# A planned attention and two-layer-pair kernel: stores on GpSimd's queue, adding transfers, packed matmuls kept together, half-size temporaries

## The chip, the cores and the metric

One core of a Trainium2 chip runs the whole program. The metric is the time of one execution on the device in microseconds; smaller is better. Engines are named as in the profile: PE is TensorE's matmul, PEld its weight load, DVE is VectorE, ACT ScalarE, POOL GpSimd, SP SyncE, which here only issues DMAs.

## The reference

```python
scores = scale * np.matmul(x, state.transpose(0, 1, 3, 2))
a = softmax(scores)
xread = np.matmul(a, state)
scores2 = scale * np.matmul(state, x.transpose(0, 1, 3, 2))
a2 = softmax(scores2)
sread = np.matmul(a2, x)
x = concat(xread, sread), laid out as 4352 tokens of 512
h = np.maximum(x @ w1, 0.0)
x = h * h @ w2
h = x @ w3
return (h / (1 + np.exp(-h))) @ w4
```

softmax stands for the reference's lines that subtract the maximum, take exp and divide by the sum. There are 8 batches with 8 heads; x has 512 rows of 64 in each head, state has 32 (S = 512, Ns = 32). The weights are 512x2048 and 2048x512. They arrive as 64-bit floats, so each weight is read as two 32-bit words.

## The kernel before, in words

**Precision.** PE multiplies in a reduced fp32 format (fp32r). A factor is therefore split into a rounded part hi (made by ACT) and a remainder lo (made by DVE or POOL), and a product is hi·hi + hi·lo + lo·hi: three matmuls of 512 columns. Some products run in plain fp32 on a part of the array instead.

**Stage one** walks through steps (batch b, column block c). For the first three batches (NB = 3) the sixteen column blocks are done in two halves (PARTS): blocks 0 to 7 for batches 0, 1, 2, then blocks 8 to 15. Since xread is a times state, the kernel first forms G = state·w1 (`g_unit`, L579: sixteen units, each with two packs of four fp32 matmuls of 64x64 on quarters of the array), and then multiplies the softmax by G (`gemm1`, L767), applies the squared ReLU (`chain_a`), and multiplies by w2 (`gemm2`, L791). The scores of the first three batches are packs of four fp32 matmuls too (`scores`, L641, tile xTr). G for batches 0 and 1 is copied straight from SBUF to SBUF (Glo<-go); the rest of G goes to DRAM (g<-go) and is loaded later (Glo<-g). The results of stage one, combined for a Strassen-like scheme of seven products, go to DRAM as the x operands (x_d, in `evac_a`, L820: seven stores for each of nine blocks).

**Conversion of weights** (`sched_conv`, L540): 32 pairs of 512 KB loads (raw), ACT takes an absolute value (cv), DVE runs seven instructions on the bits (`c_bits`, L505), which leave two fp32 parts: c (tile cc) and a small a (tile cv). `c_sum` (L523) adds them for w1, w3 and w4. `c_split` (L533) takes c apart for w2: hi by ACT, c - hi, and then lo = that + a. The converted w1 (w1d), w3 and w4 are stored to DRAM.

**Stages two and three** (`gemm3`, L968, and `gemm4`, L1034) multiply by w3 and w4, seven products each, with the intermediate t in DRAM between them.

**The order** of all engines is written by a planner at build time (`Plan`). Every call is recorded with a cost and dependencies, and `order` (L220) simulates the engines, the free tiles and the DMA lanes, picking the next instruction by earliest start and urgency; `emit` (L371) issues in that order. So a change of costs or of a queue can move any instruction. Each engine, and SP's queue, then runs its own instructions strictly in order. Because every call passes through one recorded function, nearly all rows of the profile stand at L186, and tile names tell them apart. An operation that two engines can do (`arith` on DVE or POOL, `copy` on ACT or DVE) is recorded with `either`, and the planner chooses.

**Memory.** SBUF tiles are 50 pages of 4 KB in each partition and 10 quads of 2 KB. A page whose last reader is a store comes free when the store has landed.

Of the kernel before, what the change touches and what calls it, by code (L numbers as in the profile page):

```python
# [27 lines left out]
class Plan:  # L28
# [6 lines left out]
    LATENCY = dict(act=dict(act=153, dve=147, pool=159, pe=265, dma=0),  # L35
                   dve=dict(act=128, dve=127, pool=155, pe=256, dma=0),
                   pool=dict(act=150, dve=150, pool=150, pe=309, dma=0),
                   pe=dict(act=197, dve=196, pool=200, pe=3, dma=0),
                   dma=dict(act=0, dve=0, pool=0, pe=100, dma=0))
    LANES = 8  # L40
    WINDOW = 25
# [9 lines left out]
    def __init__(self, bufs):  # L51
        self.bufs = bufs
        self.ops = []
        self.tiles = {}
        self.seen = {}
        self.slot = 0

# [49 lines left out]
    def cost(self, eng, method, writes, reads, args):  # L107
        size = 1
        for ap in writes + reads:
            n = 1  # L110
            for d in ap.shape[1:]:
                n *= d
            size = max(size, n)
        psum = any(self.tiles.get(ap.tensor.name, (0, 0, ""))[2] == "ps" for ap in writes + reads)
        if eng == "dma":
# [26 lines left out]
    def record(self, calls):  # L142
# [45 lines left out]
        self.ops.append(dict(forms=forms, deps=deps, uses=uses, slot=self.slot, port=port))  # L188

    def urgency(self, when=None):  # L190
# [3 lines left out]
        for i, o in enumerate(ops):  # L194
            if o["forms"][0][0] == "dma":
                cost[i] += self.LEAD
        late, t = [], 0.0
        for i, o in enumerate(ops):
            if o["forms"][0][0] == "pe":
                t = when[i] + cost[i] if when else t + cost[i]  # L200
                late.append(t)
            else:
                late.append(t + (self.DSLACK if o["forms"][0][0] == "dma" else self.SLACK))
# [16 lines left out]
    def order(self, when=None):  # L220
# [26 lines left out]
        ready = {e: [] for e in now}  # L247
# [8 lines left out]
        lanes, hw, wire = [], 0.0, 0.0  # L256
        port = dict(dve=0.0, pool=0.0)
        head = 0
        busy, warm = deque(), False

# [3 lines left out]
        def earliest(i, eng):  # L264
            o = ops[i]
            e = now[eng]
# [16 lines left out]
            if eng == "dma":  # L283
                e = max(e, hw)
                if len(lanes) >= self.LANES:
                    e = max(e, lanes[-self.LANES])
# [3 lines left out]
        while done < n:  # L290
# [4 lines left out]
            for eng, cand in ready.items():  # L295
                mine = []
                low = None
                for _, i in cand[:60]:
                    if ops[i]["slot"] > limit:
                        continue  # L300
                    e = earliest(i, eng)
                    if e is None:
                        continue
                    if len(ops[i]["forms"]) > 1:
                        fin = {f[0]: (earliest(i, f[0]) + f[1] - self.FAVOR[f[0]]) for f in ops[i]["forms"]}
                        if fin[eng] > min(fin.values()):
# [3 lines left out]
                    if e <= now[eng] + self.PATIENCE[eng]:  # L310
                        break
                for e, i in mine:
                    if e <= low + self.PATIENCE[eng]:
# [16 lines left out]
            if eng == "pe":  # L330
# [4 lines left out]
                end[i] = now[eng] = e + cost * (1 if warm else 2)  # L335
                if busy and e - busy[-1][1] < 10:
                    busy[-1][1] = end[i]
                else:
                    busy.append([e, end[i]])
            elif eng == "dma":  # L340
                hw = e + 450
                now[eng] = e + 60
                wire = max(wire, e + 1100) + cost
                end[i] = wire + 1500
                lanes.append(end[i])
# [4 lines left out]
            for t in o["uses"]:  # L350
                users_left[t] -= 1
                seems = e + self.DMA_SEEMS if eng == "dma" else end[i]
# [10 lines left out]
    def best(self):  # L363
        when, found = None, None
        for _ in range(self.ROUNDS):
# [12 lines left out]
def attn_moe_moe_kernel(  # L378
# [35 lines left out]
    T, D = plan.engine("pe", nc.tensor), plan.engine("dma", nc.sync)  # L414
# [65 lines left out]
    def fire(s, phase):  # L480
        for fn, a in ev.pop((s, phase), ()):
            fn(*a)

# [39 lines left out]
    def c_sum(key, into=None):  # L523
        a, c = cv[key]
        arith(ALU.add, c, c, a)
# [4 lines left out]
    def c_store(key, dst):  # L530
        D.dma_start(dst, cv[key].rearrange("p (k n) -> p k n", k=2))

    def c_split(key, into):  # L533
        a, c = cv.pop(key)
        hi, lo = page(f"hi{key}"), page(f"lo{key}")
        split_into(hi, c, c)
        arith(ALU.add, lo, c, a)
        into[key] = (hi, lo)

    def sched_conv(key, srcs, s, into=None, dst=None, ahead=3, whole=False):  # L540
# [5 lines left out]
        else:  # L546
            at(s + 2, "vec", c_split, key, into)
# [31 lines left out]
    def g_unit(i):  # L579
# [61 lines left out]
    def scores(b, g):  # L641
# [3 lines left out]
        if b < NB:  # L645
            for l in range(2):
                for r in range(2):
                    h, ps = 2 * l + r, slice(r * 64, (r + 1) * 64)
                    T.matmul(out=t[h * NS:(h + 1) * NS], lhsT=st[ps, b // 2, 2 * g + l, b % 2],
                             rhs=x[ps, l * 512:(l + 1) * 512], start=True, stop=True, tile_position=(r * 64, h * NS))  # L650
            return
# [168 lines left out]
    def evac_a(s, j, n):  # L820
# [16 lines left out]
        for i in SEQ:  # L837
            at(s + 1, "dma", lambda i=i: D.dma_start(x_d[(i, j)].rearrange("(k p) n -> p k n", p=P), v[SRC_B[i]]))
# [195 lines left out]
    def gemm4(q):  # L1034
# [20 lines left out]

        def add(o, banks, a):
            for b in range(c):
                V.tensor_tensor(out=o[:, b], in0=banks[b], in1=a[:, b], op=ALU.add)

        def join(z, a):  # L1060
            arith(ALU.add, z, a[:, :, 0:256], a[:, :, 256:512])
# [13 lines left out]
        U = new("U4")  # L1075
        for b in range(c):
            A.copy(U[:, b], BA[b])
# [3 lines left out]
        R = new("R4")  # L1081
        for b in range(c):
            A.copy(R[:, b], BA[b])
        join(z[0][:, :, ls], R)
        prod(7, BD, True, False)
        W = new("W4")
# [5 lines left out]
        X = new("X4")  # L1092
# [143 lines left out]
    base = A_END + 2  # L1236
    for u in range(NU):
# [60 lines left out]
```

## Time and profile before

| what | value |
|---|---|
| median of 3 runs | 1383.2 us (1381.34 to 1383.8) |
| the profiled execution, its own time | 1381.88 us |
| its span, first to last instruction | 1380.1 us |
| PE busy | 1335.8 us (97%) |
| DVE, ACT, POOL busy | 1056.3, 701.0, 48.9 us |
| DMA issues from POOL | none |
| mean granted TensorE clock | 0.996 of full |

The span leaves out 1.8 us of the execution's own time around it. PE busy is the time in which some matmul is on the way; it says nothing of how much of the array it uses. In a timeline a row can stand for several instructions (x8), and the bracket holds the idle time of the engine before it and what ended it. A plain fp32 matmul shows as two records, so a pack of four shows as x8.

### The profile page before, as it was taken

What the parts mean: (1) busy time and instruction counts of PE and PEld (TensorE: products, weight loads), DVE (VectorE), ACT (ScalarE), POOL (GpSimd) and SP (SyncE); (2) the same over time, 40 slices, a digit from 0 to 9 for tenths busy, and PEclk for the clock granted to TensorE, in tenths of its full rate; (3) what the DMA queues carried; (4) which work ended last, traced back from release to release, by engine and by line L of the source; (5) the groups of instructions that cost most, each with busy time, mean ns of one, the idle gap of its engine ahead of it and who ended that gap; (6) DMA issues with size and microseconds to landing.
All of it is one profiled execution on the core that took longest, in us unless ns stands there. A gap on an engine that the chain in (4) does not pass through costs nothing. (4 is left out here: it accounts for less than half of the span.)

```text
span 1380.1 us, 19261 instructions
## 1 busy us (share of the span) xinstructions
PE 1335.8 (97%) x6892; PEld 1107.9 (80%) x6892; DVE 1056.3 (77%) x1598; ACT 701.0 (51%) x1080; POOL 48.9 (4%) x41
## 2 busy tenths in 40 slices
PE   5889999999999999999999999999998999999998
PEld 1457588888888888888988888999787888888887
DVE  6979488878898888875898866777887676665664
ACT  5755776555555646554662434244455444344442
POOL 0000001110000000000020000000111000000000
PEclk9999999999999999999999999999999999999999
DMA  8761764436264546342759956667899666665663
GB/s 302 262 244 62 223 219 131 123 120 216 80 198 127 168 144 194 112 153 107 225 177 328 363 208 233 248 233 255 280 338 362 195 215 231 220 204 187 201 205 114
DMA packets 206959, 283.08 MB, mean 205 GB/s; under 512 B 13456, under 2 KB 148112, under 8 KB 206864
## 3 DMA queue, kind: packets, MB, share of 16 engines
q1 hardware_dynamic: 206864, 281.86, 61.4%
q8 instruction: 54, 0.88, 0.3%
q14 instruction: 41, 0.34, 0.1%
HBM read 161.35 MB, written 116.26 MB: 201 GB/s over the span
## 5 line engine op out<-in xcount | busy, mean ns | idle before, releaser
L186 ACT ACTIVATE rg<-psC 128x512 f32<-128x512 f32 (+1 forms) x144 | 82.6, 574 | 199.0 <-PE psC L186 195.6
L186 PE MATMUL psC<-AThi,Ghi 128*128 128x512 f32 x256 | 101.6, 400 | 6.0 <-ACT rg L186 3.1
L186 DVE TENSOR_TENSOR gact<-rg,gact 128x512 fp32r<-128x512 f32 (+1 forms) x139 | 90.9, 656 | 19.0 <-ACT rg L186 12.8
L186 PE MATMUL psC<-ATlo,Ghi 128*128 128x512 f32 x256 | 101.1, 398 | 2.2 <-DVE ATlo L186 2.2
L186 PE MATMUL psC<-AThi,Glo 128*128 128x512 f32 x256 | 101.1, 399 | 1.7 <-DVE Glo L186 1.7
L186 ACT ACTIVATE gact<-rg 128x512 fp32r<-128x512 f32 (+1 forms) x144 | 87.7, 609 | 6.9 <-DMA g<-go 3.4
L186 DVE TENSOR_TENSOR rg<-rg 128x512 f32<-128x512 f32 (+1 forms) x66 | 43.7, 662 | 48.4 <-ACT rg L186 48.0
L186 PEld LDWEIGHTS psC<-AThi,Ghi 128*128 128x128 f32 x256 | 48.1, 188 | 21.4 <-ACT AThi L186 4.6
L186 DVE TENSOR_TENSOR W<-psD,U 128x512 f32<-128x512 f32 (+2 forms) x57 | 35.4, 631 | 35.9 <-PE psD L186 35.8
L186 PEld LDWEIGHTS psC<-AThi,Glo 128*128 128x128 f32 x256 | 48.0, 188 | 16.2 <-issue 3.3
L186 PEld LDWEIGHTS psC<-ATlo,Ghi 128*128 128x128 f32 x256 | 48.2, 189 | 14.8 <-DVE ATlo L186 2.9
L186 ACT ACTIVATE r<-r 128x1024 f32<-128x1024 f32 (+2 forms) x20 | 18.6, 932 | 73.3 <-DVE r L186 61.8
L186 DVE TENSOR_SCALAR cv<-cv 128x1024 f32<-128x1024 f32 (+1 forms) x64 | 43.4, 686 | 8.2 <-ACT cv L186 7.9
L186 ACT ACTIVATE rg<-rg 128x512 f32<-128x512 f32 (+1 forms) x78 | 46.3, 594 | 0.0
L186 DVE TENSOR_TENSOR U<-psB,U 128x512 f32<-128x512 f32 (+2 forms) x57 | 35.0, 629 | 14.1 <-PE psB L186 12.6
L186 DVE TENSOR_TENSOR W<-psC,U 128x512 f32<-128x512 f32 (+2 forms) x40 | 24.2, 609 | 27.6 <-PE psC L186 27.2
L186 ACT ACTIVATE cv<-raw 128x512 f32<-128x512 f32 x64 | 40.7, 668 | 8.9 <-DMA raw<-in_w_dram 8.9
L186 PE MATMUL psA<-cc,st 64*64 64x512 f32 x128 | 25.9, 641 | 17.7 <-DVE cc L186 17.3
L186 DVE SCALAR_TENSOR_TENSOR cc<-raw,cv 128x512 int32<-128x512 int32 x64 | 41.9, 684 | 1.4 <-DMA g<-go 1.2
L186 DVE SCALAR_TENSOR_TENSOR cv<-raw,cv 128x512 f32<-128x512 uint32 x64 | 41.5, 682 | 0.2
L186 DVE TENSOR_TENSOR Glo<-Glo,Ghi 128x1024 fp32r<-128x1024 f32 x31 | 37.7, 1216 | 1.2 <-ACT Ghi L186 1.0
L186 ACT COPY U<-psA 128x512 f32<-128x512 f32 (+2 forms) x57 | 28.9, 538 | 14.9 <-PE psA L186 14.3
(1244 smaller groups left out, 4276.2 us busy)
## 6 DMA issues: line engine op xcount, KB each, us to landing
raw<-in_w_dram SPq DMA_DIRECT2D x64, 512.0 KB, 6.4
t<-s SPq DMA_DIRECT2D x36, 512.0 KB, 5.0
Glo<-g SPq DMA_DIRECT2D x96, 128.0 KB, 4.6
t<-r SPq DMA_DIRECT2D x24, 512.0 KB, 4.6
xTr<-in_xT_dram SPq DMA_DIRECT2D x16, 512.0 KB, 8.3
g<-go SPq DMA_DIRECT2D x16, 512.0 KB, 5.7
xnr<-in_xN_dram SPq DMA_DIRECT2D x16, 512.0 KB, 5.6
x<-yt SPq DMA_DIRECT2D x32, 256.0 KB, 4.0
```

The costliest lines, as they stand in the source:

```text
L186: lambda engine=engine, method=method, a=a, k=k: getattr(engine, method)(*a, **k)))
```

## The change

- The queue: the stores of G (g_d), of converted weights (w1_d, w3_d, w4_d) and of the x operands (x_d) are issued by GpSimd (`DS`) instead of SP (`D`). Loads, the copies Glo<-go, the stores of t and of the output stay on SP. `arith` in stage one is DVE's alone; from stage two on either engine's.
- The sums: `c_sum` is a transfer from SBUF to SBUF that adds, for all pairs but w1's 3 and w2's 0. For w2, `c_sum` now runs ahead of `c_split`, which then needs one DVE instruction less.
- The packs: the four matmuls of a pack of G or scores form a group, which the planner starts when all members are ready and issues back to back; their model cost is no longer divided by the packing.
- Copies of G's units 0 to 7 out of PSUM (tile go) are ACT's alone.
- The temporaries U, R, W, X of `gemm4` are quads, one for each of the c row blocks, instead of one page; `join` is issued once for each of them.
- The planner models the second queue (1000 ns per issue).

```diff
+    DMA = ("dma", "sdma")
     LANES = 8
+    ISSUE = 1000
...
-            share = 128 * 128 // (reads[0].shape[0] * writes[0].shape[0]) if args.get("tile_position") else 1
-            return max(n / 2.4 + 13, 109) * (4 if args["rhs"].dtype == F32 else 1) / share
+            return max(n / 2.4 + 13, 109) * (4 if args["rhs"].dtype == F32 else 1)
...
-                for _, i in cand[:60]:
-                    if ops[i]["slot"] > limit:
+                for _, i in [key[m] for m in rest] if eng == "pe" and rest else cand[:60]:
+                    if ops[i]["slot"] > limit and i not in rest:
                         continue
-                    e = earliest(i, eng)
+                    g = ops[i]["group"]
+                    if g is not None and i not in rest:
+                        if any(left[m] for m in self.members[g]):
+                            continue
+                        e = max(earliest(m, eng) for m in self.members[g])
+                    else:
+                        e = earliest(i, eng)
...
-    T, D = plan.engine("pe", nc.tensor), plan.engine("dma", nc.sync)
+    T = plan.engine("pe", nc.tensor)
+
+    D, DS = plan.engine("dma", nc.sync), plan.engine("sdma", nc.gpsimd)
...
+    pool_stores = [True]
+
     def arith(op, o, a, b):
         kw = dict(out=o, in0=a, in1=b, op=op)
-        plan.either((V, "tensor_tensor", kw), (G, "tensor_tensor", kw))
+        if pool_stores[0]:
+            V.tensor_tensor(**kw)
+        else:
+            plan.either((V, "tensor_tensor", kw), (G, "tensor_tensor", kw))
...
     def c_sum(key, into=None):
         a, c = cv[key]
-        arith(ALU.add, c, c, a)
+        if key in (("w1", 3), ("w2", 0)):
+            arith(ALU.add, c, c, a)
+        else:
+            DS.dma_start(c, a, accum_op=ALU.add)
...
     def c_store(key, dst):
-        D.dma_start(dst, cv[key].rearrange("p (k n) -> p k n", k=2))
+        DS.dma_start(dst, cv[key].rearrange("p (k n) -> p k n", k=2))
 
     def c_split(key, into):
-        a, c = cv.pop(key)
+        c = cv.pop(key)
         hi, lo = page(f"hi{key}"), page(f"lo{key}")
-        split_into(hi, c, c)
-        arith(ALU.add, lo, c, a)
+        split_into(hi, lo, c)
         into[key] = (hi, lo)
...
         else:
+            at(s + 1, "vec", c_sum, key)
             at(s + 2, "vec", c_split, key, into)
...
+            plan.together = ("G", i, bp)
             for k in range(2):
                 for r in range(2):
...
+            plan.together = None
...
-                copy(o2[:, k], ts[k])
+                (A.copy if 4 * q < PARTS[0][1] else copy)(o2[:, k], ts[k])
...
-                D.dma_start(g_d[q][0][p], o2[:, 1])
+                DS.dma_start(g_d[q][0][p], o2[:, 1])
             else:
-                D.dma_start(g_d[q][1][p], o2)
+                DS.dma_start(g_d[q][1][p], o2)
 
     def w1_store(i):
-        D.dma_start(w1_d[i], w1p.pop(("w1", i)))
+        DS.dma_start(w1_d[i], w1p.pop(("w1", i)))
...
+            plan.together = ("scores", b, g)
...
-            at(s + 1, "dma", lambda i=i: D.dma_start(x_d[(i, j)].rearrange("(k p) n -> p k n", p=P), v[SRC_B[i]]))
+            at(s + 1, "dma", lambda i=i: DS.dma_start(x_d[(i, j)].rearrange("(k p) n -> p k n", p=P), v[SRC_B[i]]))
...
+        def quads_of(name):
+            return [quad(f"{name}{b}") for b in range(c)]
+
...
         def join(z, a):
-            arith(ALU.add, z, a[:, :, 0:256], a[:, :, 256:512])
+            for b in range(c):
+                arith(ALU.add, z[:, b], a[b][:, 0:256], a[b][:, 256:512])
...
-        U = new("U4")
+        U = quads_of("U4")
...
+    pool_stores[0] = False
     for u in range(NU):
```

## Rows read from the trace of the kernel before

**Rows 1.** The page: its span, and the busy time and share of each engine.

```profile
span 1380.1 us, 19261 instructions
...
PE 1335.8 (97%) x6892; PEld 1107.9 (80%) x6892; DVE 1056.3 (77%) x1598; ACT 701.0 (51%) x1080; POOL 48.9 (4%) x41
```

**Rows 2.** The table by stages: stretch, its length, then busy time by engine, clock, DMA.

```profile
0.00:35.00 35.00, 18.50 (x108) 4.88 (x108) 22.06 (x34) 19.21 (x33) 2.48 (x8) 1.00 0.82 301
...
35.00:69.00 34.00, 27.60 (x128) 15.68 (x127) 31.65 (x50) 25.32 (x45) 0.00 (x0) 1.00 0.79 262
...
69.00:138.00 69.00, 60.18 (x236) 42.75 (x235) 60.99 (x99) 36.38 (x65) 1.25 (x2) 0.95 0.41 153
...
138.00:966.00 828.00, 827.25 (x4225) 700.06 (x4225) 656.93 (x1090) 440.69 (x727) 30.71 (x23) 1.00 0.58 191
...
966.00:1104.00 138.00, 132.94 (x664) 111.06 (x662) 108.24 (x127) 69.79 (x93) 14.46 (x8) 1.00 0.86 294
...
1104.00:1380.00 276.00, 269.33 (x1541) 233.48 (x1539) 176.48 (x201) 109.58 (x123) 0.00 (x0) 0.99 0.61 197
```

**Rows 3.** PE's timeline to 140 us: start, duration, instruction, the wait before it.

```profile
14.86 1.99 PE L186 MATMUL psA<-cc,st 64*64 64x512 f32 x8 [14.86 <-DVE cc L186]
...
48.01 0.73 PE L186 MATMUL psC<-AThi,Ghi 128*128 128x512 f32 x2 [1.68 <-ACT AThi L186]
...
94.91 1.22 PE L186 MATMUL psC<-ATlo,Ghi 128*128 128x512 f32 x2 [2.21 <-DVE ATlo L186]
```

**Rows 4.** DVE's timeline to 140 us.

```profile
27.61 0.69 DVE L186 COPY go<-psB 128x512 f32<-128x512 f32 x1 [5.66 <-PE psB L186]
...
74.77 1.23 DVE L186 TENSOR_TENSOR cc<-cc,hi('w2', 2)_324 128x1024 f32<-128x1024 f32 x1 [4.20 <-ACT hi('w2', 2)_324 L186]
...
97.72 2.49 DVE L186 TENSOR_SCALAR cv<-cv 128x1024 f32<-128x1024 f32 x4
```

**Rows 5.** The waits of ACT from 45 to 100 us: total, times, longest.

```profile
ACT Ghi L186 <- DMA w1d<-cc: 2.2, 1, 2.2
...
ACT hi('w2', 2)_324 L186 <- DMA g<-go: 2.0, 1, 2.0
```

**Rows 6.** SP's timeline to 110 us: start, time for all issues of the row.

```profile
35.49 15.32 SPq L186 DMA_DIRECT2D Glo<-go  x22
...
50.85 3.94 SPq L186 DMA_DIRECT2D g<-go  x6
```

**Rows 7.** The groups of instructions on DVE, whole run, then up to 138 us: busy us, mean ns.

```profile
L186 DVE TENSOR_TENSOR cc<-cc,cv 128x1024 f32<-128x1024 f32 x24 | 29.0, 1218 | 0.1
...
L186 DVE TENSOR_TENSOR lo('w2', 1)_307<-cc,cv 128x1024 fp32r<-128x1024 f32 x1 | 1.2, 1221 | 0.0
...
L186 DVE TENSOR_TENSOR cc<-cc,cv 128x1024 f32<-128x1024 f32 x8 | 9.6, 1218 | 0.0
```

**Rows 8.** DMA issues up to 100 us: count, KB each, median us to landing.

```profile
raw<-in_w_dram SPq DMA_DIRECT2D x24, 512.0 KB, 8.1
...
Glo<-go SPq DMA_DIRECT2D x32, 64.0 KB, 2.1
```

**Rows 9.** PE's timeline again: packs of G and of scores.

```profile
25.56 1.09 PE L186 MATMUL psA<-cc,st 64*64 64x512 f32 x8
...
26.47 1.04 PE L186 MATMUL psB<-cc,st 64*64 64x512 f32 x8
...
73.14 1.04 PE L186 MATMUL psD<-xTr,st 64*32 64x512 f32 x2
...
78.33 0.50 PE L186 MATMUL psC<-AThi,Glo 128*128 128x512 f32 x1
...
79.89 1.06 PE L186 MATMUL psD<-xTr,st 64*32 64x512 f32 x8
```

**Rows 10.** The table for the second half of G alone.

```profile
139.95:158.86 18.91, 18.91 (x134) 5.90 (x133) 4.75 (x7) 14.32 (x28) 0.00 (x0) 1.00 0.65 196
```

**Rows 11.** The chain that ended last, from 940 to 1110 us.

```profile
1039.83 9.19 DMA t<-s
```

More of the change, by code (lines that the diff above doesn't have):

```diff
@@ L56, in __init__ @@
         self.slot = 0
+        self.together = None
     def tile(self, pool, shape, dt, tag, name, space="sb"):
@@ L114, in cost @@
         psum = any(self.tiles.get(ap.tensor.name, (0, 0, ""))[2] == "ps" for ap in writes + reads)
-        if eng == "dma":
+        if eng in self.DMA:
             n = 1
@@ L187, in record @@
         port = {c[0]: self.shares(c[0], writes, reads) for c in calls}
-        self.ops.append(dict(forms=forms, deps=deps, uses=uses, slot=self.slot, port=port))
+        self.ops.append(dict(forms=forms, deps=deps, uses=uses, slot=self.slot, port=port,
+                             group=self.together if eng == "pe" else None))
     def urgency(self, when=None):
@@ L194, in urgency @@
         for i, o in enumerate(ops):
-            if o["forms"][0][0] == "dma":
+            if o["forms"][0][0] in self.DMA:
                 cost[i] += self.LEAD
@@ L198, in urgency @@
         for i, o in enumerate(ops):
+            if o["group"] is not None:
+                cost[i] /= len(self.members[o["group"]])
             if o["forms"][0][0] == "pe":
@@ L202, in urgency @@
             else:
-                late.append(t + (self.DSLACK if o["forms"][0][0] == "dma" else self.SLACK))
+                late.append(t + (self.DSLACK if o["forms"][0][0] in self.DMA else self.SLACK))
         before = [list(o["deps"]) for o in ops]
@@ L246, in order @@
         now = dict(pe=600.0, act=1900.0, dve=1070.0, pool=1150.0, dma=600.0)
-        ready = {e: [] for e in now}
+        clock = dict({e: e for e in now}, sdma="pool")
+        ready = {e: [] for e in clock}
         def add(i):
@@ L259, in order @@
         busy, warm = deque(), False
+        rest, begun = [], 0.0
         def fresh(i):
@@ L265, in earliest @@
             o = ops[i]
-            e = now[eng]
+            e = begun + 7 if i in rest else now[clock[eng]]
             for d in o["deps"]:
@@ L282, in earliest @@
                 e = max(e, port["pool" if eng == "dve" else "dve"])
[L283 to L286, printed above, removed]
+            if eng in self.DMA:
+                e = max(e, hw[eng])
+                if len(lanes[eng]) >= self.LANES:
+                    e = max(e, lanes[eng][-self.LANES])
             return e
@@ L334, in order @@
                 warm = work > (1000 if warm else 2400)
-                end[i] = now[eng] = e + cost * (1 if warm else 2)
+                end[i] = e + cost * (1 if warm else 2)
+                now[eng] = max(now[eng], end[i])
+                if o["group"] is not None:
+                    rest, begun = [m for m in rest or self.members[o["group"]] if m != i], e
                 if busy and e - busy[-1][1] < 10:
-                    busy[-1][1] = end[i]
+                    busy[-1][1] = max(busy[-1][1], end[i])
                 else:
                     busy.append([e, end[i]])
[L340 to L343, printed above, removed]
+            elif eng in self.DMA:
+                issue = 450 if eng == "dma" else self.ISSUE
+                hw[eng] = e + issue
+                now[clock[eng]] = e + (60 if eng == "dma" else issue)
+                wire = max(wire, e + 650 + issue) + cost
                 end[i] = wire + 1500
-                lanes.append(end[i])
+                lanes[eng].append(end[i])
             else:
@@ L351, in order @@
                 users_left[t] -= 1
-                seems = e + self.DMA_SEEMS if eng == "dma" else end[i]
+                seems = e + self.DMA_SEEMS if eng in self.DMA else end[i]
                 last_end[t] = max(last_end[t][0], seems), max(last_end[t][1], end[i])
@@ L364, in best @@
         when, found = None, None
+        self.members = defaultdict(list)
+        for i, o in enumerate(self.ops):
+            if o["group"] is not None:
+                self.members[o["group"]].append(i)
         for _ in range(self.ROUNDS):
@@ L650, in scores @@
                              rhs=x[ps, l * 512:(l + 1) * 512], start=True, stop=True, tile_position=(r * 64, h * NS))
+            plan.together = None
             return
@@ L1080, in gemm4 @@
         prod(2, BA, False, True)
-        R = new("R4")
+        R = quads_of("R4")
         for b in range(c):
-            A.copy(R[:, b], BA[b])
+            A.copy(R[b], BA[b])
         join(z[0][:, :, ls], R)
         prod(7, BD, True, False)
-        W = new("W4")
+        W = quads_of("W4")
         add(W, BD, U)
@@ L1091, in gemm4 @@
         prod(4, BD, False, True)
-        X = new("X4")
+        X = quads_of("X4")
         add(X, BD, U)
```

21 lines of the change are left out of this document (11 added, 10 removed).

## The prediction

> **What bounds the kernel now.** I began with the page's busy shares: TensorE (PE) is busy for 1335.8 of 1380.1 us, so at most 44.3 us of idle PE time is there to win, and GpSimd (POOL) is nearly empty [rows 1]. The table by stages shows where the idle time lies. PE lacks 16.5, 6.4 and 8.8 us in the three stretches up to 138 us, 0.75 us in the 828 us behind them, 5.1 us between 966 and 1104, and 6.7 us after that, most of it the last store [rows 2]. From 138 to 966 us PE alone is the bound; there only a shorter PE stream helps. In the opening, VectorE (DVE) is the full engine: 31.65 of 34 us, then 60.99 of 69 [rows 2]. PE's own timeline names the same engine: its first matmul waits 14.86 us for the converted weights cc, and the waits at 48.01 and 94.91 end with AThi and ATlo, which stand behind DVE's work [rows 3].
>
> DVE isn't full of useful work, though. It stands still for 5.66 us before a copy of go, which the order gave to it and which waits for PE, and for 4.20 us before a subtraction that needs hi(w2,2) from ScalarE (ACT) [rows 4]. ACT was late there because a page came free only when a store of go (2.0 us), and before that a store of w1d (2.2 us), had landed [rows 5]. Those stores sat in SyncE's (SP's) queue behind 22 issues of Glo<-go that took from 35.49 to 50.85 us; the first store of go went out at 50.85 us [rows 6], long after its copy.
>
> **Part 1, the sums.** The kernel makes 24 sums cc<-cc,cv and 8 sums lo(w2)<-cc,cv on DVE, 1.22 us each [rows 7]. 30 of the 32 become adding transfers, 36.6 us of DVE time. Where PE is the bound (w3, w4 and late w2: 20 of them) this is worth nothing: PE's full rows hide it, and without that cover it would be worth the 1.22 us each. In the opening it counts: three sums of w1 and three of w2 lie ahead of the last PE wait at 94.91 us, 6 x 1.22 = 7.3 us. Four more (w1 pairs 4 to 7, the rest of the eight up to 138 us [rows 7] but pair 3) come before 138 us, 4.9 us against PE waits of about 2 us there (the rest of the 8.8 us lies ahead of 97 us): I take 2.0.
>
> What they cost has no row: no transfer here adds. From below, a 64 KB copy from SBUF to SBUF landed in 2.1 us; from above, twice the 8.1 us of a 512 KB load, since it reads both operands, 16.2 us [rows 8]. I take 8.1, the row of the same size in the same crowded stretch (DMA share 0.82 and 0.79 [rows 2]). So each sum is late by 8.1 - 1.2 = 6.9 us on two chains in turn, weights to G at the head and w2 to its products: 13.8 us if nothing covers it, 0 if DVE always has another pair's bits to work on. The next pair's steps (seven of about 0.69 us) are ready in most places, and the sums of pair 3 of w1 and pair 0 of w2 stay on DVE; I charge 4.
>
> **Part 2, stores on POOL's queue.** 119 stores (32 of go, 24 of weights, 63 of x operands) leave SP, and with the 30 sums POOL issues 149. At 1 us each (the diff's own ISSUE; SP took 15.32 us for 22, 0.7 each [rows 6]) POOL holds some 150 us of issues over 966 us, one by one: a store behind a sum that waits for DVE waits too, and so does the page that it holds. SP's queue keeps the loads and Glo<-go. The wait for pages at 74.77 us should mostly go; next late there is ACT's own queue, so I count 2.0 of the 4.20. POOL's tensor work moves to DVE: 30.71 us in 23 instructions in the stage from 138 to 966 [rows 2], under half of that on DVE, which is busy for 657 of 828 us there; hidden behind PE, cost 0. Without that cover it would be about 15 us, less than the 24 us of sums that leave the same stage.
>
> **Part 3, copies of go on ACT for the first eight units.** The stall of 5.66 us and the copy (0.69 us) leave DVE [rows 4]. ACT takes one copy more, in a stretch where it is busy for 19.21 of 35 us. Together 6.3.
>
> **Part 4, packs kept together.** A pack is four fp32 matmuls on parts of the array. Kept together, eight records of G pass in 0.91 us (25.56 to 26.47) and a pack of scores in 1.06. Where other matmuls came between, a pack of scores lasted from 73.14 to 78.33, 5.2 us: 3.4 lost, with 0.7 taken off for the other matmuls in it [rows 9]. The second half of G takes 18.91 us from 139.95, in a stretch with PE full [rows 10]; 16 whole packs at 0.91 are 14.6 and six other matmuls some 1.4, so 2.9 us are lost: I count 3.0. The pack of scores lies in the part that DVE bounds: 0 to 3.4, I take 0. A pack starts only when all four are ready, at most one copy of a bank later (0.69 us), and other products fill PE.
>
> **Part 5, half-size temporaries.** They leave six pages per round of the last product stage for two. In the chain that ended last, U waits 9.19 us for the store t<-s at 1039.83 [rows 11]; but PE lacks only 5.1 us in this whole stretch [rows 2], and loads at a DMA share of 0.86 are late next. Between 0 and 3.6, I take 1. Smaller additions cost DVE some us more after 1104, hidden behind PE (269.33 of 276 us).
>
> **The sum.** Opening: 7.3 + 6.3 + 2.0 - 4.0 = 11.6; then 2.0, 3.0 and 1.0: 17.6 us. The profiled execution took 1381.9 us and so comes to 1364.3; the median of the runs, 1383.2, is 1.3 us above it. I say 1365. PE has room for the opening's share: 31.7 - 14.9 = 16.8 us of waits behind its first matmul [rows 2, 3], the split packs, and a mean granted clock of 0.95 of its upper level, 2.4 GHz, from 69 to 138 us, where it had waited before [rows 2].
>
> **The rivals.** *Late sums* (0.22): the 13.8 us aren't covered, because DVE's order reaches a step that needs a sum and stands. Then 17.6 - 9.8 = 7.8 us remain, 1374 (1370 to 1379.5). For it: DVE has four tensor_scalar at a stretch (2.49 us [rows 4]) that POOL may have to share memory with, and the loads of the first stretch crowd the DMA engines. Against it: most of DVE's order is conversions that don't depend on each other. On this the Trainium skill (SBUF — State Buffer, "SBUF: two separate sides") says that a DMA issued from GpSimd can't have its descriptors written while such a VectorE instruction holds the shared port pair, and advises SyncE's or ScalarE's queue; no run here shows it yet. By that rule each sum would be up to 2.5 us later, and this rival gains at the forecast's cost.
>
> *Slower* (0.09): the sums take the upper bound. One mechanism: both chains late by 16.2 - 1.2 = 15 us, uncovered, 30 us against gains of 17.6 + 4 = 21.6; +8.4, 1390. It decides from a landing of 1.2 + 21.6/2 = 12 us. Only the assumption that adding doubles a transfer speaks for it.
>
> *More* (0.12): all sums covered (+4), the whole 4.20 (+2.2), the scores' pack (+3.4) and the late 2.6 more: 29.8 us, 1352 (1350 to 1358).
>
> *No effect* (0.07): the order is planned anew for the whole kernel, the freed DVE time is spent on conversions that nobody waits for, and new waits take the pack's 3 us: 1380.5 to 1386. The skill's page DMA: Bandwidth & Descriptors ("Issuing engines are not separate DMA queues") says that a second issuing engine saves only issue time. By it alone part 2 would give its 2.0 us or less; SP's 15.32 us block [rows 6] says that here the issue time is what held the stores.
>
> **How the numbers follow.** The forecast (1358 to 1370) has 0.50. The range 1353 to 1381 leaves out the slower case, most of no effect and a piece of more, together 0.2. A difference of 0.2% (2.8 us) is about what can be told from none: faster has 0.50 + 0.22 + 0.12 = 0.84, same 0.07, slower 0.09.
>
> **What would show it.** Right: PE idle up to 138 us falls from 31.7 to 25 or less though its first matmul on G comes later than 14.86 us; no copy of go on DVE before 60 us; stores of go issued before 40 us; an adding transfer landing in 5 to 10 us; scores and G in whole packs, the second half of G in some 16 us; 138 to 966 still without PE waits. Wrong: adding transfers over 12 us; PE waiting for lo(w2) or for G by several us at a time; DVE's tensor_scalar longer than 0.69 us while POOL issues; or new PE waits after 138 us.

## The result, and the profile after

| | before | changed |
|---|---|---|
| median of 4 runs, us | 1383.5 (1381.34 to 1385.19) | 1366.73 (1365.78 to 1370.45) |
| ratio | | 0.9885, 95% interval 0.9862 to 0.9908 |

By the ratio the changed kernel is faster by 15.9 us, 1.15%. It was run again as the first experiment, with a median of 1366.9, and its rows are read from that profile: the execution took 1367.0 us, at the median, while the first one profiled was the longest of its four.

First the page of the changed kernel: the span and the busy times (against [rows 1]), the queue that GpSimd's issues go to, and the adding transfers among the DMA issues (count, KB each, median us from issue to landing).

```profile
span 1365.2 us, 19493 instructions
...
PE 1323.6 (97%) x6892; PEld 1104.5 (81%) x6892; DVE 1041.7 (76%) x1637; ACT 692.8 (51%) x1067; POOL 126.7 (9%) x166
...
q0 software_dynamic: 16176, 56.50, 14.1%
...
cc<-cv POOLq DMA_DIRECT2D x30, 512.0 KB, 7.1
```

PE's idle time went from 44.3 to 1365.2 - 1323.6 = 41.6 us, 2.7 us less. The other 12.2 us of the gain in the span are PE *busy* time, although the count of matmuls is the same: the stream itself passes faster. DVE lost 36.6 us of sums and is down by only 14.6: work came back to it, 22 us in net, and what left POOL and the smaller additions are the likely part of that. POOL, busy for 48.9 us with tensors before, is now busy for 126.7 us, mostly with issues, and its queue (q0) holds the DMA engines for 14.1% of their time.

The same table by stages as [rows 2] says where:

```profile
0.00:35.00 35.00, 10.80 (x64) 2.18 (x64) 26.21 (x42) 12.06 (x19) 8.66 (x16) 1.00 0.98 344
35.00:69.00 34.00, 25.65 (x141) 12.25 (x138) 27.52 (x44) 28.23 (x53) 10.78 (x17) 0.95 1.02 344
69.00:138.00 69.00, 68.50 (x322) 51.17 (x324) 59.03 (x106) 44.87 (x78) 8.24 (x12) 1.00 0.64 177
138.00:966.00 828.00, 825.55 (x4209) 699.67 (x4199) 649.24 (x1092) 430.60 (x709) 94.33 (x118) 1.00 0.65 206
966.00:1104.00 138.00, 137.98 (x712) 117.31 (x711) 114.30 (x143) 75.37 (x95) 4.74 (x3) 1.00 0.89 297
```

Up to 138 us PE is idle for 24.2 + 8.35 + 0.5 = 33.1 us, more than the 31.7 of before. The first stretch got worse (10.80 us busy against 18.50), with DMA now full at 0.98 where it was 0.82. From 69 to 138 us PE is busy for 68.50 us and passes 322 matmuls, where it passed 236 in 60.18 [rows 2]. The mix differs (36 of the 322 are short records of G), so the counts alone mislead; with each matmul at its full-rate time (as set out below) 66.5 us of work begin in this stretch, against 51.2 before. So PE passes 0.97 us of work in a busy microsecond in place of 0.85. A pack that other matmuls split counts as busy throughout, so this gain shows in the work passed and not in the idle time; a part of it is the clock, 1.00 against 0.95 (before, PE is busy for 5.3 us at the lower of the two levels, 1.2 GHz, so some 2.7 us at most). From 966 to 1104 us the 5.1 us of idle time are gone.

PE's timeline shows the head (start, duration, tiles, and in brackets the wait before it):

```profile
11.72 3.64 PE L188 MATMUL psD<-xTr,st 64*32 64x512 f32 x16 [11.72 <-DMA xTr<-in_xT_dram]
27.49 1.93 PE L188 MATMUL psD<-xTr,st 64*32 64x512 f32 x8 [12.14 <-DMA xTr<-in_xT_dram]
29.35 1.66 PE L188 MATMUL psA<-cc,st 64*64 64x512 f32 x8
...
53.13 1.67 PE L188 MATMUL psB<-cc,st 64*64 64x512 f32 x7 [2.97 <-ACT go L188]
...
58.06 0.73 PE L188 MATMUL psC<-AThi,Ghi 128*128 128x512 f32 x2
```

G starts at 29.35 us instead of 14.86, and the first product with the softmax at 58.06 instead of 48.01 [rows 3]. The queues of SP and POOL say why:

```profile
11.60 1.74 SPq L188 DMA_DIRECT2D xTr<-in_xT_dram  x2
...
32.68 33.35 SPq L188 DMA_DIRECT2D Glo<-go  x24
```

```profile
14.36 1.06 POOL L188 DMA_DIRECT2D cc<-cv  x1 [11.26 <-DVE cv L188]
...
31.97 0.55 POOL L188 DMA_DIRECT2D g<-go  x1 [4.65 <-ACT go L188]
```

The first sum is issued at 14.36 us, into DMA engines full of loads of raw, and lands some 10 us later (the median up to 35 us is 10.1, shown with the second experiment). The new order has the scores of the next batch ahead of G on PE. Their operand xTr, issued at 11.60, lands at 27.5, and PE, which works in order, stands for 12.14 us. The first store of go, in return, leaves at 31.97 us from POOL while SP begins its Glo<-go: before, it left at 50.85 [rows 6].

**Time by equal work.** Since idle time misleads here, I compared the two traces where they have done the same work: each matmul is given the time that it needs at full rate (its columns at 2.4 GHz plus 13.5 ns, which for 512 columns is the 0.227 us at which such matmuls follow each other in the trace, and 0.11 us for a record of a fp32 pack, eight in about 0.91 us), the sums run up in the order of the matmuls' starts, and the times at which both reach the same sum are subtracted. At the sum that before had reached at 42.4 us the changed kernel is 10.7 us *behind*; at 84.2 it is 3.9 behind; at 104.3 it is 6.3 ahead and at 161.7 it is 9.1 ahead; this stays to 1014.0 (8.0 ahead); then 12.6 at 1069.1 and 15.9 at 1323.3. So the time came in two places: between 84 and 138 us, and after 1014 us.

### The profile page after: what moved, and what is told of

It reads as the page before. It is cut to its first block, busy times and chain, and to the rows that moved or that the text cites. A ratio compares the mean times of both kernels' runs of the same rounds, so it can differ in the third digit from the quotient of the medians.

```text
span 1368.7 us, 19493 instructions
## 1 busy us (share of the span) xinstructions
PE 1325.1 (97%) x6892; PEld 1104.2 (81%) x6892; DVE 1042.7 (76%) x1637; ACT 691.4 (51%) x1067; POOL 126.2 (9%) x166
## 4 chain that ended last, share of the span: by engine, by line
PE 88%; DMA 7%; ACT 1%; issue 1%; DVE 1%; SPq 1%; POOL 0%; DVEq 0%; POOLq 0%; ACTq 0%
PE psA L188 26%; PE psC L188 26%; PE psB L188 20%; PE psD L188 16%; DMA raw<-in_w_dram 3%; DMA xTr<-in_xT_dram 1%; SPq L188 1%; DMA cc<-cv 1%; DMA x44lo<-x 1%; ACT go L188 0%; DMA g<-go 0%; POOL g L188 0%; DMA w<-w4s 0%; DMA out_dram<-z 0%; DMA x47lo<-x 0%
## 5 line engine op out<-in xcount | busy, mean ns | idle before, releaser
L188 DVE TENSOR_TENSOR gact<-rg,gact 128x512 fp32r<-128x512 f32 (+1 forms) x144 | 94.3, 656 | 24.3 <-ACT rg L188 14.8
L188 DVE TENSOR_TENSOR rg<-rg 128x512 f32<-128x512 f32 (+1 forms) x73 | 49.1, 672 | 56.6 <-ACT rg L188 55.6
L188 DVE TENSOR_SCALAR cv<-cv 128x1024 f32<-128x1024 f32 (+1 forms) x64 | 44.0, 695 | 12.8 <-ACT cv L188 12.5
L188 POOL DMA_DIRECT2D cc<-cv x30 | 27.5, 919 | 259.7 <-DVE cv L188 120.9
L188 ACT ACTIVATE cv<-raw 128x512 f32<-128x512 f32 x64 | 41.1, 674 | 18.1 <-DMA raw<-in_w_dram 18.1
L188 DVE TENSOR_TENSOR U<-psB,U 128x512 f32<-128x512 f32 (+2 forms) x57 | 35.7, 629 | 14.5 <-PE psB L188 10.7
L188 ACT ACTIVATE rg<-rg 128x512 f32<-128x512 f32 (+1 forms) x71 | 41.5, 585 | 0.1
L188 ACT ACTIVATE r<-psA 128x512 f32<-128x512 f32 (+2 forms) x40 | 21.1, 535 | 31.9 <-PE psA L188 30.9
```

What stands on the lines that cost most here:

```text
L188: lambda engine=engine, method=method, a=a, k=k: getattr(engine, method)(*a, **k)))
```

## The experiments

All were timed in rounds against the kernel before. "Saved" is one minus the ratio, times the median of before in the same call. The last columns are the difference to before by equal work, in us, from the profiled executions, at the work that before had done at these times.

| run | median, us | ratio and interval | saved, us | 161.7 | 459.9 | 1069.1 | 1323.3 |
|---|---|---|---|---|---|---|---|
| e1_again | 1366.9 | 0.9887 (0.9864 to 0.991) | 15.6 | -9.1 | -8.4 | -12.6 | -15.9 |
| e2_copy_for_add | 1361.8 | 0.9849 (0.9833 to 0.9865) | 20.9 | -14.9 | -14.2 | -19.0 | -22.3 |
| e3_sums_on_dve | 1366.6 | 0.9884 (0.9869 to 0.99) | 16.0 | -9.4 | -8.4 | -12.5 | -15.8 |
| e4_stores_on_sp | 1369.8 | 0.9911 (0.9893 to 0.9929) | 12.3 | -7.1 | -5.3 | -9.5 | -12.8 |
| e5_pages_again | 1374.3 | 0.9933 (0.9917 to 0.995) | 9.3 | -7.2 | -6.3 | -9.7 | -11.4 |
| e6_packs_loose | 1375.0 | 0.9945 (0.993 to 0.996) | 7.6 | +0.1 | +0.1 | -4.7 | -8.0 |
| e7_w1_sums_dve | 1366.6 | 0.9883 (0.9858 to 0.9909) | 16.2 | -12.9 | -12.0 | -15.8 | -19.1 |
| e8_all_sums_dve | 1364.1 | 0.9868 (0.9851 to 0.9884) | 18.3 | -11.6 | -11.1 | -15.6 | -19.0 |
| e9_copies_free | 1367.9 | 0.9896 (0.988 to 0.9912) | 14.4 | -8.4 | -7.5 | -11.4 | -14.7 |
| e10_hybrid | 1363.6 | 0.9869 (0.9851 to 0.9887) | 18.1 | -12.8 | -11.9 | -13.2 | -16.4 |
| e11_only_halves | 1373.8 | 0.9937 (0.9918 to 0.9956) | 8.7 | +0.6 | +0.6 | -3.2 | -6.6 |
| e12_only_packs | 1376.3 | 0.9956 (0.9941 to 0.997) | 6.1 | -8.1 | -7.6 | -5.7 | -5.6 |

An interval is 2 to 3.5 us to either side. The last columns are of single executions: those of e2, e5 and e7 were 1.5, 3.0 and 2.9 us faster than their medians, those of e10 and e11 2.6 and 1.5 slower. e1 to e4 keep the order of the changed kernel; the others are planned anew, and that adds a scatter of its own. e5, for one, edits only tiles of the last stage, but its opening has another order and is 1.9 us worse at 161.7; by this one case a planned run tells its part to about 2 us.

The granted clock differs between the openings too: up to 69 us e3's profile is at a mean of 0.85 of the upper level, e2's at 1.00. In e3 it doesn't show in the time: runs at mean clocks of 0.991 and 0.996 took 1366.75 and 1366.72 us. Only e7's runs part with it.

### The changed kernel again (e1_again)

No edit.

> The changed kernel once more, for a second profile. Laid beside the kernel before by equal PE work, the first profile (1370.45 us, the longest of its four runs) had the opening 6 us earlier, the second half of G no earlier, and the stretch from 1014 to 1069 us 5 us earlier. If the four other microseconds of the median lie in the opening, whose transfers crowd the DMA engines, this profile shows the opening 9 to 11 us earlier and everything behind it as in the first. If they lie elsewhere, the opening is again 6 us earlier.

Measured: 1366.9 us, 15.6 saved. At 161.7 us this profile is 9.1 us ahead, as expected if the difference lies in the opening, where the first was 7.8; but it also gains more behind that, 6.8 us against 5.4. It is what the next three are compared with.

### A copying transfer in place of the adding one (e2_copy_for_add)

```diff
-            DS.dma_start(c, a, accum_op=ALU.add)
+            DS.dma_start(c, a)
```

> The same order of every engine; the 30 transfers copy cv over cc instead of adding it, so the converted weights lack c (the sum is left out) and the output is another. Theory A (the sums off DVE pay, and the length of the transfers is covered): 1366.7, within 2 us. Theory B (the opening is now bound by the DMA engines, on which a packet of an adding transfer takes 327 ns and a plain one 160 to 184): the landing falls from 10 us to 6 in the first 35 us, and the kernel is 2 to 5 us faster, 1362 to 1365.

The order, the queues and the bytes written are the same; the sum is left out. It took 1361.8 us, 5.1 less than the changed kernel, and nearly all of the profile's difference is there at 161.7 us (-14.9 against -9.1). The table of stages for 14 to 26 us, the changed kernel first and then this one (the last two columns are the DMA share and GB/s):

```profile
14.00:26.00 12.00, 1.36 (x8) 0.00 (x0) 12.00 (x21) 5.08 (x8) 2.32 (x3) 1.00 1.04 305
```

```profile
14.00:26.00 12.00, 2.61 (x16) 0.23 (x8) 12.00 (x20) 5.05 (x8) 2.21 (x3) 1.00 1.03 396
```

And the DMA issues up to 35 us, in the same order:

```profile
q0 software_dynamic: 575, 2.10, 22.3%
...
cc<-cv POOLq DMA_DIRECT2D x3, 512.0 KB, 10.1
```

```profile
q0 software_dynamic: 593, 2.17, 15.1%
...
cc<-cv POOLq DMA_DIRECT2D x3, 512.0 KB, 7.5
```

The DMA engines are full in both (1.04 and 1.03), but with adds in the stream they move 305 GB/s and with copies 396. About as many packets on GpSimd's queue hold the engines for 22.3% of their time in place of 15.1%. An adding transfer isn't only late itself, it takes bandwidth from the loads beside it. PE's timeline shows it on xTr, for which PE stood until 27.49 us; with copies it lands 3 us earlier:

```profile
24.52 1.93 PE L188 MATMUL psD<-xTr,st 64*32 64x512 f32 x8 [9.39 <-DMA xTr<-in_xT_dram]
```

Nothing but the adding is gone in this run, and 5.1 us with it.

### The same order, the sums on DVE (e3_sums_on_dve)

```diff
+    class OnVector:
+        def dma_start(self, c, a, accum_op):
+            nc.vector.tensor_tensor(out=c, in0=c, in1=a, op=accum_op)
+
+    DV = plan.engine("sdma", OnVector())
...
-            DS.dma_start(c, a, accum_op=ALU.add)
+            DV.dma_start(c, a, accum_op=ALU.add)
```

> The same order of PE, ACT and SP; at the place of each adding transfer DVE adds, 30 x 1.22 us. Theory A: the opening loses the seven to ten sums that lie ahead of 100 us, 7 to 12 us slower, 1374 to 1379. Theory B: in the opening the transfer's 10 us were worse than DVE's 1.22, and the kernel is as fast or up to 5 us faster, 1362 to 1367.

1366.6 against 1366.9 us, and the same difference at every station (within 0.3 us). 30 additions put back on DVE, at places that were chosen for transfers, cost what the transfers cost, though at other places. The load xTr lands 5.6 us earlier than in the changed kernel:

```profile
21.85 1.93 PE L188 MATMUL psD<-xTr,st 64*32 64x512 f32 x8 [6.71 <-DMA xTr<-in_xT_dram]
```

But PE then waits 3.14 us for scores (Sc) and 2.27 us for Glo, and at the work of 60.0 us it is 10.3 us behind the kernel before, the changed kernel 9.8. So in this order the head is late without the transfers too, and taking the sums off DVE is worth nothing.

### The same order, the stores on SP (e4_stores_on_sp)

```diff
+    DP = plan.engine("sdma", nc.sync)
...
-                DS.dma_start(g_d[q][0][p], o2[:, 1])
+                DP.dma_start(g_d[q][0][p], o2[:, 1])
...
-        DS.dma_start(w1_d[i], w1p.pop(("w1", i)))
+        DP.dma_start(w1_d[i], w1p.pop(("w1", i)))
```

(and the other three places that store)

> The same order of all engines; the 119 stores are issued by SP at the same places, the sums stay on GpSimd. By the prediction's part 2 (pages come free late behind Glo<-go in SP's queue) some 2 us slower, and the waits of ACT for pages are back. Rival 1: nothing (within 1 us), since the planner's order already spreads them. Rival 2: 5 us or more, since SP's queue, which Glo<-go holds from 32.3 to 66.1 us, also holds the loads behind it.

1369.8 us: 2.8 more. In ACT's waits from 30 to 100 us (total, times, longest) it stands at

```profile
ACT Ghi L188 <- DMA Glo<-go: 6.3, 2, 4.6
```

On one queue the Glo<-go stand behind the stores; Ghi is late, and PE stands for 5.2 us for it, until 59.02 us. On two queues PE has no such wait. The Trainium skill (DMA: Bandwidth & Descriptors, "Issuing engines are not separate DMA queues") says that a second issuing engine saves only issue time. The trace agrees for the most part: in the chain of work up to 66 us SP issues one transfer after another from 51.20 to 55.3 us, a store of go, three Glo<-go, a store of w1d and the last Glo<-go, which lands at 57.7. Some issues also wait with others behind them in the queue (for copies of go 5.3 us in seven places from 30 to 66 us); how the 2.8 us divide isn't shown. The order was planned for two queues, so an order made for one might lose less.

### The pages again (e5_pages_again)

```diff
         def quads_of(name):
-            return [quad(f"{name}{b}") for b in range(c)]
+            t = new(name)
+            return [t[:, b] for b in range(c)]
```

> The changed kernel with U, R, W and X in pages as before (planned anew). Theory A (the half-size temporaries removed the waits for pages between 1014 and 1069 us, and a little in each later round): that stretch is 4 to 5 us longer again and the last product stage up to 2 us, 1371 to 1374, with PE waits before the products of w4 back. Rival (the new order of the rest did it): within 1.5 us of 1366.9.

9.3 us saved, 6.3 less than the changed kernel. The profiled execution, the fastest of its four, is behind by 4.5 us at 1323.3; 1.9 of these are lost in the opening (161.7 us), and 2.4 behind 459.9 us. PE's waits after 966 us (total, times, longest), in before, in this kernel, and in the changed one:

```profile
PE psA L186 <- ACT U L186: 2.8, 5, 0.9
PE psD L186 <- DVE W L186: 1.9, 2, 1.3
PE psD L186 <- ACT g070hi L186: 0.9, 1, 0.9
PE psD L186 <- DVE g070lo L186: 0.5, 1, 0.5
```

```profile
PE psA L188 <- ACT U L188: 1.9, 3, 1.0
PE psD L188 <- ACT g070hi L188: 1.2, 1, 1.2
```

```profile
PE psC L188 <- DVE W L188: 0.2, 1, 0.2
```

6.1 us of waits before, 3.1 here, 0.2 with half-size temporaries. They are for U and W themselves and for an operand (g070) of the last products.

### The packs loose (e6_packs_loose)

```diff
-            return max(n / 2.4 + 13, 109) * (4 if args["rhs"].dtype == F32 else 1)
+            share = 128 * 128 // (reads[0].shape[0] * writes[0].shape[0]) if args.get("tile_position") else 1
+            return max(n / 2.4 + 13, 109) * (4 if args["rhs"].dtype == F32 else 1) / share
...
-            plan.together = ("G", i, bp)
+            plan.together = None
...
-            plan.together = ("scores", b, g)
+            plan.together = None
```

> The changed kernel without the groups, with the packing in the model's cost as before (planned anew). By the prediction 3 us slower in the second half of G. What the two profiles show by equal work: the second half of G gained only 0.3 us, since each switch between a pack and other products costs some 0.2 us; the gain of the packs was that of the scores near 73 us (3.4 us). So by that: 2 to 5 us slower, 1369 to 1372, with split scores in the timeline, and the second half of G within 1 us. Rival: the groups themselves made the first scores and G late at the head (PE waits for all four), and without them the head is 3 us or more earlier: 1360 to 1365.

7.6 us saved: 8.0 are lost, more than expected, and all of them in the opening (level with the kernel before at 161.7 us, where the change is 9.1 ahead). By equal work 3 us are lost by 124.3 and 7 by 138.0, ahead of the second half of G, and under 2 in that half; from 124 to 138 us PE waits 1.41 us for AThi and passes 3.4 us at the lower clock, which it doesn't in the changed kernel. PE's timeline in the second half of G, here and in the changed kernel:

```profile
138.25 1.07 PE L189 MATMUL psA<-cc,st 64*64 64x512 f32 x2
...
139.68 0.65 PE L189 MATMUL psA<-cc,st 64*64 64x512 f32 x3
...
142.20 0.65 PE L189 MATMUL psB<-cc,st 64*64 64x512 f32 x2
```

```profile
131.66 1.09 PE L188 MATMUL psA<-cc,st 64*64 64x512 f32 x8
...
133.34 1.09 PE L188 MATMUL psB<-cc,st 64*64 64x512 f32 x8
...
152.25 1.04 PE L188 MATMUL psB<-cc,st 64*64 64x512 f32 x8
```

Packs begin piecemeal (x2, x3) when loose and are whole (x8) when kept together. With whole packs the half still lasts from 131.66 to some 155 us, because other products come between the packs.

### More sums back on DVE, planned anew (e7_w1_sums_dve, e8_all_sums_dve)

e7:

```diff
-        if key in (("w1", 3), ("w2", 0)):
+        if key in (("w1", 0), ("w1", 1), ("w1", 2), ("w1", 3), ("w2", 0)):
```

> The sums of the first four pairs of w1 are DVE's (planned anew, so the order knows of it). Theory B (the head is late by the adding transfers, 10 us each in a full stretch of DMA, and by PE standing 12 us before the scores of batch 1, which the order put ahead of G): the first G comes at 15 to 19 us in place of 29, and the kernel is 3 to 8 us faster, 1359 to 1364. Theory A (DVE's time is what counts): 3.7 us slower, 1370. Rival: the head is bound elsewhere (copies of go on ACT, Glo<-go on SP), G earlier, the time within 2 us.

e8:

```diff
-        if key in (("w1", 3), ("w2", 0)):
+        if True:
```

> All 32 sums are DVE's again (planned anew), everything else as in the changed kernel. Theory A: 7 to 12 us slower, 1374 to 1379. Theory B: as good as the run before or the changed kernel, 1360 to 1367, since the opening no longer waits for DVE once the stores and the copies of go are off its way.

e7 saved 16.2 us, as its rival expectation has it (the time within 2 us). Its four runs part: 1363.7 and 1364.2 us at mean granted clocks of 0.996 and 0.995, 1370.3 and 1369.0 at 0.992 and 0.991; the profile is of the fastest, and why they part isn't known. e8 saved 18.3. Without any adding transfer the change is better by 2.7 us in the saving. The intervals of the two ratios overlap, but the longest run of e8 (1365.63 us) is below the shortest of the changed kernel (1365.78). The head is back, in PE's timeline of e8:

```profile
14.45 1.99 PE L188 MATMUL psA<-cc,st 64*64 64x512 f32 x8 [14.45 <-DVE cc L188]
...
44.28 1.22 PE L188 MATMUL psC<-AThi,Ghi 128*128 128x512 f32 x2 [7.00 <-ACT AThi L188]
```

G starts 15 us earlier and the first product 13.8. But PE then waits 7.00 us for AThi, later 3.00 for hi(w2,3) and 3.01 for gact: by equal work the lead over the changed kernel is 12.8 us at 84.2, 6.3 at 104.3 and 2.5 at 161.7. Most of a head regained is lost to the next chains.

### The copies of go on either engine (e9_copies_free)

```diff
-                (A.copy if 4 * q < PARTS[0][1] else copy)(o2[:, k], ts[k])
+                copy(o2[:, k], ts[k])
```

> The changed kernel with the copies of go left to the planner's choice of ACT or DVE, as before (planned anew). By the prediction (5.66 us of stall and 0.69 of copy): some 6 us slower, 1373, with a copy of go on DVE ahead of 60 us and DVE idle before it. Rival: since the changed head waits for transfers and for ACT's copies of go (PE's waits at 35.7, 39.3, 46.4 and 53.1 us), a DVE that takes some of them helps it: 2 to 4 us faster, 1363 to 1365. New orders have moved the opening by some 2 us either way, so less than that tells nothing.

14.4 us saved, 1.2 less, which the interval doesn't tell from nothing; neither expectation came. Where the planner may choose again, two of these copies are DVE's up to 60 us, and no stall like the one of [rows 4] comes back with them.

### The sums of the opening on DVE, the others by transfer (e10_hybrid)

```diff
-        if key in (("w1", 3), ("w2", 0)):
+        if key in [(n, i) for n in ("w1", "w2") for i in range(4)]:
```

> The sums of w1's and w2's first four pairs are DVE's, the other 24 are adding transfers. If what an adding transfer costs is the crowded DMA of the first 70 us, and what it gives is DVE time around 118 us (where the kernel with all sums on DVE has PE wait 3.0 us for gact), this has the better of both: 1360 to 1363, against 1364.1 for all sums on DVE and 1366.9 for the changed kernel. Rival: the place of a sum doesn't matter anywhere, 1364 to 1367.

18.1 us saved: nothing beyond e8. The other 24 sums may be made either way.

### Two parts by themselves (e11_only_halves, e12_only_packs)

e11 is the kernel before with:

```diff
+        def quads_of(name):
+            return [quad(f"{name}{b}") for b in range(c)]
...
-            arith(ALU.add, z, a[:, :, 0:256], a[:, :, 256:512])
+            for b in range(c):
+                arith(ALU.add, z[:, b], a[b][:, 0:256], a[b][:, 256:512])
...
-        U = new("U4")
+        U = quads_of("U4")
```

(R, W and X likewise)

> The kernel before with the half-size temporaries alone (planned anew). Theory: the opening as before (within 2 us), the stretch from 1014 to 1069 us shorter by 2 to 5 us, the rounds behind it by 1 to 2 us: 1376 to 1379. Rival: the late gain of the changed kernel is of its new order, not of the temporaries: within 2 us of the kernel before.

e12 is the kernel before with the planner's groups, and nothing else of the change:

```diff
-            share = 128 * 128 // (reads[0].shape[0] * writes[0].shape[0]) if args.get("tile_position") else 1
-            return max(n / 2.4 + 13, 109) * (4 if args["rhs"].dtype == F32 else 1) / share
+            return max(n / 2.4 + 13, 109) * (4 if args["rhs"].dtype == F32 else 1)
...
+            plan.together = ("G", i, bp)
...
+            plan.together = ("scores", b, g)
```

> The kernel before with the groups and their model cost alone (planned anew). By the prediction (3.0 us in the second half of G, 0 to 3.4 for the scores): 1377 to 1380. By the run with the packs loose (8 us slower than the changed kernel): 1373 to 1377. Rival: with DVE the bound of the opening, nothing: within 2 us of the kernel before.

The half-size temporaries alone save 8.7 us, more than expected, and by equal work all of it is after 1014 us. The table of stages and PE's waits after 966 us of e11:

```profile
966.00:1104.00 138.00, 136.47 (x693) 115.72 (x692) 115.81 (x140) 75.74 (x98) 11.66 (x7) 1.00 0.92 308
```

```profile
PE psA L186 <- ACT U L186: 1.5, 1, 1.5
PE psC L186 <- DVE W L186: 0.2, 1, 0.2
```

29 more matmuls pass in the stage (664 in [rows 2]), and 1.7 us of waits are left of 6.1. These 4.4 us are about half of the 8.2 gained by equal work from 1014 us on; for the rest I have no row. The packs alone save 6.1 us; by equal work they are 8.1 us ahead at 161.7 us and give 2.5 of it back later. On the way there they are 8.5 us ahead at 45.2 and only 1.0 at 60.0, after a wait of PE of 3.77 us for rg and 6.8 us at the lower clock. From 73.0 to 78.5 us they gain 3.6: there the kernel before splits a pack of scores (73.14 to 78.33 [rows 9]). The changed kernel gains 3.7 at this place, and e6 3.6, whose order has no scores there. The timelines of DVE in e11 and in e12 tell what became of the stall of [rows 4]:

```profile
28.67 0.69 DVE L186 COPY go<-psB 128x512 f32<-128x512 f32 x1 [6.75 <-PE psB L186]
```

```profile
21.73 0.69 DVE L188 COPY go<-psA 128x512 f32<-128x512 f32 x1 [0.18 <-PE psA L188]
```

It is still there with the halves alone (6.75 us) and gone with the packs alone (0.18), though the copy is on DVE as before. Together the two parts save 14.8 us singly: nearly the whole change.

## Why the prediction was right, and which of its terms were wrong

The forecast was 1365 and the kernel takes 1366.7, inside the range. The sum was right because its errors cancelled, which was luck; term by term:

| part | predicted, us | taken back out of the change | by itself |
|---|---|---|---|
| sums by transfer | 7.3 + 2.0 - 4.0 = 5.3 | 0 (e3), -2.7 (e8) | not tried |
| copies of go on ACT | 6.3 | 1.2 (e9) | not tried |
| stores on POOL's queue | 2.0 | 2.8 (e4) | not tried |
| packs kept together | 3.0 | 8.0 (e6) | 6.1 (e12) |
| half-size temporaries | 1.0 | 6.3 (e5) | 8.7 (e11) |

**The sums, wrong.** The step "In the opening it counts: 6 x 1.22 = 7.3 us" took DVE's busy share for the bound of the opening. A copy in the transfer's place saves 5.1 us (e2), and DVE adding at the same places costs nothing (e3). The landing was sized well (8.1 taken, 7.1 over the run, 10.1 up to 35 us; none over 12). What the step left out is the bandwidth: it priced the lateness of one transfer, not the loads that an adding transfer slows. The 4 us charged for lateness were too few for the head, which came 10 us later; but e3, in the same order, has it as late without the transfers, so the landing alone doesn't explain it. The rival *late sums* had the mechanism, but at another engine and price: PE, not DVE, stood (12.14 us), and the loss was made up behind it.

**The copies, wrong.** The step "The stall of 5.66 us and the copy leave DVE" was true of the rows and false of the cause: the stall goes as soon as the packs are kept together (e12). And e6, with these copies on ACT and the packs loose, is level with before at 161.7 us. Which engine copies is worth 1.2 us by e9, not told from nothing. I put the wait down to who copied; it was due to when PE would have finished. That loose packs made the planner expect PE too early is the likely reason; groups and their model cost weren't tried apart, so this is argued, not shown.

**The stores, right** in size (2.0 against 2.8) and in place: first store of go at 31.97 us, predicted before 40.

**The packs, right in kind, undersized and misplaced.** The 3.0 us were to come from the second half of G in "some 16 us"; it takes about 24, with other products between the packs. By equal work that half (138.0 to 161.7) is 0.1 us shorter in the changed kernel and 0.8 in e12. The gain came earlier: e12 is 7.3 us ahead at the work that before had done at 124.3 us. The scores, for which I had taken 0 of 0 to 3.4 because DVE bounds that part, are in it with the 3.6 us of the pack at 73.14: the upper end came, and PE, not DVE, was the bound there. The head, with the stall above gone, gave 8.5 us, most of which was lost again by 60 us; what of it is left in the end isn't told apart.

**The half-size temporaries, undersized.** Between 0 and 3.6 I took 1, because loads at a DMA share of 0.86 were to be late next. They weren't: the share rose to 0.89 (0.92 in e11) and PE's waits after 966 us went from 6.1 us to 0.2. The upper end itself was too low: the whole 5.1 us of the stage should have been the bound, and the stage behind it gained too (3.4 us of e11's from 1069 to 1323). How much of the late gain in the changed kernel is its new order isn't settled: with pages again, e5 still keeps part of it.

**The list of what would show it.** Right: no copy of go on DVE before 60 us, scores and G in whole packs. Wrong: PE idle up to 138 us didn't fall to 25 (33.1), since the gain was in PE's busy time; PE stood 12.14 us for xTr, a wait that the list doesn't have; and from 138 to 966 us PE's idle time rose a little, from 0.75 to 2.45 us. Of the feared 2.5 us per sum no more than a part came. An issue of an adding transfer takes 0.92 us on the mean; with a tensor_scalar of DVE beside it 1.02 (6 cases), without 0.89 (24), and tensor_scalar on cv takes 694 ns (686 before). The Trainium skill's rule (SBUF — State Buffer, "SBUF: two separate sides") would have the writing of descriptors wait for DVE; in the issues 0.1 us each shows here. From issue to landing the six took 8.5 us on the mean and the others 7.4; as two of the six lie in the full stretch of the head, this isn't told apart from the load.

## What to carry to other kernels

A busy engine in a full stretch is not yet its bound: look at the DMA share and at what a moved operation takes from the transfers beside it, and compare versions by the time at equal work, since split packs and slow orders count as busy time. Where a planner writes the order, try every part alone and taken back out, and expect a scatter from the new order itself (some 2 us here). Here the change without its adding transfers (e8) is as good as any version that makes the sums, at 1364.1 us.

## What was unexpected of the hardware

- A packet of 4096 bytes took 328 ns in an adding transfer and 159 ns in a copy of the same tiles (medians): here adding about doubled the time that the DMA engines were held. Over the whole run the 30 transfers landed in 7.1 us when adding and in 5.3 when copying (medians), and this was worth 5.1 us of the kernel.
- Whole packs of G back to back begin 0.91 us apart [rows 9]; between them and the full-array products there is a loss: from a lone pack in the second half to the next matmul it is 1.02 us, and the pack itself starts 0.1 to 0.2 us later behind a full-array matmul than another full one would. This would explain why keeping packs whole but alternating them with other products won little there.
- In both kernels one stretch of the opening shows a mean granted clock of 0.95 of the upper level: 69 to 138 us before (6.8 us at the lower level, from 93.4), 35 to 69 us after (3.4 us, from 54.4), each after PE had waited. From 69 us on the changed kernel has 1.00.
